# Attention output computed transposed: values as 32-column weights, and no moves or turns of the output

## The chip, the core and the metric

The kernel runs on one NeuronCore of one Trainium2 chip. A core has five engines that run their own instruction streams in order: TensorE (matmuls; PE in the profile, with PEld for its weight loads), VectorE (DVE), ScalarE (ACT), GpSimd (POOL) and SyncE (SP, which here only issues transfers). They meet through semaphores. Matmul results go to PSUM, which has eight banks of 128 partitions by 512 fp32 numbers; everything else lies in SBUF. The metric is the device time of one execution in microseconds (us), the median of several runs.

## What is computed

The input is 2048 tokens of width 448. The block normalizes them, sends the result through two branches and multiplies the branches:

```python
xn = _layernorm(x)                                  # (1, 2048, 448)
q, k, v = split(xn @ wqkv)                          # 16 heads of 28
idx = pos[:, None] - 2 * arange(8)[None, :]         # 8 keys: this token and 7 earlier ones, 2 apart
logits = einsum("bhsd,bhswd->bhsw", q, k[idx]) * 28 ** -0.5   # idx < 0 masked
o = einsum("bhsw,bhswd->bhsd", softmax(logits), v[idx])
s = o.reshape(1, 2048, 448) @ wo
g = silu(gelu(xn @ w1 + b1) @ w2 + b2)              # hidden width 1792
out = x + s * g
```

So there are an attention branch with a short dilated window, a feed-forward branch that serves as a gate, and one multiplication at the end.

## The kernel before

**Layout.** Even and odd tokens are kept apart, which turns the step of 2 into a step of 1: each half is 1024 positions. The 2048 positions stand as 16 tiles of 128 (`t`) and four chunks of 512 (`c`). `xnT` holds the normalized input transposed, four slices of 128 channels each (the last holds 64 channels twice, so that two jobs with only 64 rows of contraction can run side by side in the two halves of the array).

**Projections** (L528, L531 for queries and keys; L554, L557 for values). One tile gives three outputs of 128 x 448 in PSUM, which VectorE or ScalarE cast into `qk_tok` and `v_tok` (L310, L312, one helper for both engines). Heads are padded to 32 columns there. Column 28 and those after it are 1.0 in `v_tok`, so that a product with it also gives the sum of the weights. Queries and keys are transposed by SP's transfers into `qkT`.

**Attention** works in 17 blocks: block 0 has 128 queries, the others have 120, each with 128 keys. Head h is 4g + hl. One PE task (L676) computes the scores of a block: 16 matmuls with 32 rows of contraction each, four of which (hl = 0 to 3) lie in the four row groups of the array and write to four banks. For each hl, ScalarE takes the exponential of a bank into `E` (L682), VectorE multiplies by the mask (L690), and a PE step (L698) multiplies by the values: `E` of four heads as weights of 128 columns, 29 columns of `v` moving. The results of all 16 heads of a block are one bank, with queries on partitions. Values for blocks other than those that start on a tile are moved to partition 0 by GpSimd's transfers (L354, `v<-v_tok`).

**Division and turn.** VectorE inverts the 16 sums (L705) and multiplies (L710) into `os`; GpSimd issues one or two transfers that move the rows of `os` to their place in a tile `ot` (L354, 31 in all); SP issues a transposing transfer per tile (L360, 16 in all) into `oT`, channels on partitions.

**Feed-forward.** L587 and L590 give a 128 x 512 bank of the hidden layer per column tile; ScalarE applies GELU (L594). L627 contracts over 14 tiles of the hidden layer for each token tile. Then come the bias (L649), a tanh (L655) and the gate (L659).

**End** (`final_part`). L740: four matmuls with slices of `oT` as weights and `wo` moving; L745 multiplies by the gate, L750 adds x, and SP writes out.

**What sets the order.** The order on each engine isn't that of the loops. Each piece of work is a task of a `_Plan` with an engine (or two to choose from), an estimated cost, dependencies, buffers to take and give, and a priority out of `PRIO` and `LATER`. The plan is made once in Python by list scheduling, and instructions are then issued in its order; each engine runs its own list strictly in that order. The plan knows three `mode`s of TensorE (128, 64 and 32 rows of contraction), charges 0.095 us (`SWITCH`) for going from one to another, and favours tasks of the small modes while it is in one.

ScalarE has separate function tables for GELU and for exponentials, so the plan does them in stretches: GELU of chunks 0 and 1; exponentials of the blocks of chunks 0 to 2; GELU of chunk 2; exponentials of chunk 3; GELU of chunk 3.

Of the kernel before, what the change touches and what calls it, by code (L numbers as in the profile page):

```python
# [8 lines left out]
F32 = mybir.dt.float32  # L9
BF16 = mybir.dt.bfloat16  # L10
ALU = mybir.AluOpType
# [142 lines left out]
def kernel(  # L154
# [13 lines left out]
    P = 128  # L168
# [64 lines left out]
    def ring(name, n, shape, dt=BF16, fifo=False):  # L233
        return _Pool([sb(f"{name}{i}", shape, dt) for i in range(n)], fifo)

    p_xn = ring("xn", 4, [P, 512])
    p_st = ring("st", 4, [P, 6], F32)
    p_E = ring("E", 8, [P, 4, P], fifo=True)
    p_rd = ring("rd", 2, [P, H], F32)
    p_os = ring("os", 3, [P, D])  # L240
    p_ot = ring("ot", 4, [P, 512])
    p_y = ring("y", 2, [P, D], F32)
    p_t = ring("t", 2, [P, D], F32)
    p_g = ring("g", 4, [P, D])
# [12 lines left out]

    FF1 = (((3, 3), (2, 2), (2, 2)),
           ((2, 4), (2, 2), (2, 2)),
           ((3, 3), (2, 2), (2, 2)),  # L260
           ((5, 3), (3, 3)))
    JOINED = (True, True, False, False)

    PRIO = {
                "project": (47.5, 177.5, 195, 32.5,),
                "project2": (47.5, 147.5, 83, 27,),
                "values": (19.5, 53.5, 102.5, 106.5,),
                "attn": (191.5, 153.5, 199, 129, 79, 74, 54, 45.5, 30.5, 15.5, 15, 5.5, 179, 138.5, 104, 89,
            36.5,),
                "ff1": (170.5, 149, 112, 188, 179, 171.5, 14, 154.5, 143.5, 64, 165.5, 199,),  # L270
                "gelu": (1, 169, 51, 42.5,),
                "ff2": (133.5, 156.5, 162.5, 51.5, 1, 94.5, 109, 5.5, 47, 74.5, 112.5, 31.5, 11.5, 184.5,
            58, 1,),
                "final": (178.5, 32.5, 3, 6, 4, 110, 48.5, 1, 92, 22, 20.5, 50.5, 63, 29, 52.5, 48,),
                "norm": (100.5, 67, 116.5, 168, 199, 166, 159, 131, 1, 130.5, 41, 33, 113, 169, 57.5,
            75.5,),
                "loads": (194.5, 199, 133, 114.5, 69.5,),
                "stats": (83.5, 84, 180.5, 54, 89, 43.5, 2, 115.5, 143, 141.5, 157.5, 148, 29.5, 181, 184,
            81.5,),
                "turn_x": (124, 175, 199, 48, 62, 134, 123, 137, 63, 137, 199, 48.5, 130.5, 159, 35.5,  # L280
            195,),
                "turn_qk": (81.5, 79.5, 61, 171.5, 109, 73.5, 124, 136, 91.5, 31, 33, 153.5, 36.5, 168.5,
            100.5, 24,),
                "turn_o": (1, 1, 129.5, 145.5, 138, 35.5, 137.5, 140.5, 129.5, 20.5, 20.5, 139.5, 199,
            100.5, 42, 57.5,),
                "move_v": (27, 188, 169.5, 91, 52.5, 20, 147, 148.5, 58.5, 114, 93.5, 183.5, 44.5, 57,
            162.5, 175.5, 31,),
                "move_o": (176.5, 1.5, 160.5, 173, 169.5, 165.5, 155, 52.5, 189, 56, 174.5, 118.5, 93, 195,
            135, 163, 128.5,),
                "copies": (33, 125, 87.5, 3, 162, 46, 32, 84, 83.5, 161.5, 58.5, 1.5, 6, 58.5, 167,),  # L290
    }
    LATER = {"qk": 60, "v": 41.5, "gelu": 15, "exp": 35.5, "mask": -30, "pv": -4.5, "recip": 17.5, "os": -17, "y": 7, "tanh": -23, "g": -30, "sg": 9.5, "o": -15.5}

    plan = _Plan()

    def buf(pool, owner, i=0):
        return pool.bufs[owner.slots[pool][i]]
# [4 lines left out]
    def act(n):  # L302
        return 0.15 + n / 1130.0

    def dve(n, r=1):
        return 0.15 + n / (960.0 * r)
# [8 lines left out]
    def memset(eng, ap, v):  # L315
        def fn(_):
            getattr(nc, eng).memset(ap, v)
        return fn
# [17 lines left out]

    t_qz = [plan.add("DVE", 0.08, memset("vector", q[:, :, :, DH:], 0.0), [t_on], prio=95) for q in qk_tok]
    t_vw = [plan.add("DVE", 0.08, memset("vector", v[:, :, DH:], 1.0), [t_on], prio=96) for v in v_tok[:9]]
    t_os = [plan.add("POOL", 0.1, memset("gpsimd", o[:, D:], 0.0), [t_on], prio=94) for o in p_ot.bufs]
    t_row0 = plan.add("POOL", 0.1, memset("gpsimd", row0[:], 0.0), [t_on], prio=93)  # L340
    t_row0 = plan.add("POOL", 0.1, memset("gpsimd", row0[:1, :], 1.0), [t_row0], prio=93)
    t_wo = [plan.add("POOL", 0.45, memset("gpsimd", wo[64:, 3, :], 0.0), [t_on], prio=93)]
    t_E = [plan.add("POOL", 0.1, memset("gpsimd", e[:, :, NQ:], 0.0), [t_on], prio=95) for e in p_E.bufs]

    def dma(eng, dst, src, kb, prio, deps=(), issue=0.5, rate=350.0):
        def fn(_):
# [314 lines left out]
        t_g[t].append(plan.add("DVE", dve(n), f4, [th] + after, prio + LATER["g"], take=(p_g,), give=held + ((p_t, th, 0),)))  # L661


    t_oT, ot_at = {}, {}
    ot = [[] for _ in range(NT)]

    def attn(b, prio, gate, early):
        q0, nq, k0 = BLK[b]
# [11 lines left out]
        for hl in range(4):  # L680
            def f2(k, hl=hl):
                nc.scalar.activation(buf(p_E, k)[:, :, :nq],  # L682
                                     buf(p_b, a, hl)[:, :4 * nq].rearrange("p (g q) -> p g q", g=4),
                                     ACT.Exp, scale=SCALE)
            e = plan.add("ACT", act(4 * nq), f2, [a] + gate + t_E, prio + LATER["exp"], take=(p_E,), give=((p_b, a, hl),), table=("exp",))
            exps.append(e)

            def f3(_, e=e):
                E = buf(p_E, e)
                nc.vector.tensor_tensor(out=E[:, :, :nq], in0=E[:, :, :nq], in1=m[:, :, :nq], op=ALU.mult)  # L690
            w = plan.add("DVE", dve(4 * nq, 2), f3, [e] + t_mask, prio + LATER["mask"])

            def f4(k, e=e, hl=hl):
                ps = buf(p_b, pv[0] if hl else k)[:].rearrange("p (h c) -> p h c", h=H)
                v = buf(*v_at[b]) if v_at[b] else v_tok[k0 // P]
                for g in range(G):
                    h = 4 * g + hl
                    nc.tensor.matmul(ps[:, h, :DH + 1], buf(p_E, e)[:, g, :], v[:, h, :DH + 1],  # L698
                                     start=True, stop=True)
            pv.append(plan.add("PE", 0.12, f4, [w] + t_v[b] + pv[-1:], prio + LATER["pv"], take=() if hl else (p_b,),  # L700
                               give=((p_E, e, 0),) + ((v_at[b],) if hl == 3 and v_at[b] else ()), tail=0.15))
        po = pv[0]

        def f5(k):
            nc.vector.reciprocal(buf(p_rd, k)[:nq, :],  # L705
                                 buf(p_b, po)[:nq, :].rearrange("p (h c) -> p h c", h=H)[:, :, DH])
        r = plan.add("DVE", 0.25, f5, [pv[-1]], prio + LATER["recip"], take=(p_rd,))

        def f6(k):
            nc.vector.tensor_tensor(  # L710
                out=buf(p_os, k)[:nq, :].rearrange("p (h c) -> p h c", h=H),
                in0=buf(p_b, po)[:nq, :].rearrange("p (h c) -> p h c", h=H)[:, :, :DH],
                in1=buf(p_rd, r)[:nq, :].unsqueeze(2).to_broadcast((nq, H, DH)), op=ALU.mult)
        o = plan.add("DVE", dve(D), f6, [r], prio + LATER["os"], take=(p_os,), give=((p_b, po, 0), (p_rd, r, 0)))
        q, mine = q0, []
        while q < q0 + nq:
            t, row = divmod(q, P)
            n = min(P - row, q0 + nq - q)
            first, d = dma_sb(lambda k, t=t, row=row, n=n: buf(p_ot, ot_at.get(t, k))[row:row + n, :D],
                          lambda q=q, n=n: buf(p_os, o)[q - q0:q - q0 + n, :], [o] + t_os + mine + [d for _, d in ot[t]],  # L720
                          PRIO["move_o"][b], () if ot[t] else (p_ot,), ((p_os, o, 0),) if q + n == q0 + nq else ())
            ot[t].append((first, d))
            mine = [first]
            ot_at[t] = ot[t][0][0]
            if row + n == P:
                t_oT[t] = dma_T(oT[:, :, t * P:(t + 1) * P], lambda t=t: buf(p_ot, ot_at[t])[:], [d for _, d in ot[t]], PRIO["turn_o"][t],
                                (p_ot, ot_at[t], 0))
            q += n
        return exps


# [4 lines left out]
    def final_part(t, cs, n, g, prio):  # L736
        def f1(k):
            ps = buf(p_b, k)
            for kt in range(KT):
                nc.tensor.matmul(ps[:, :n], oT[:, kt, t * P:(t + 1) * P], wo[:, kt, cs],  # L740
                                 start=(kt == 0), stop=(kt == KT - 1))
        a = plan.add("PE", pe(n, KT), f1, [t_oT[t]] + t_wo + [t_f2[t]], prio, take=(p_b,), tail=0.15)

        def f2(k):
            nc.vector.scalar_tensor_tensor(out=buf(p_sg, k)[:, :n], in0=buf(p_b, a)[:, :n], scalar=0.5,  # L745
# [1 line left out]
        s = plan.add("DVE", dve(n), f2, [a, g], prio + LATER["sg"], take=(p_sg,), give=((p_b, a, 0), (p_g, g, 0)))  # L747

        def f3(k):
            nc.vector.tensor_tensor(out=buf(p_o, k)[:, :n], in0=x_sb[:, t, cs], in1=buf(p_sg, s)[:, :n], op=ALU.add)  # L750
        o = plan.add("DVE", dve(n, 2), f3, [s], prio + LATER["o"], take=(p_o,), give=((p_sg, s, 0),))

        def f4(_):
            nc.sync.dma_start(rows(o_half, t * P, P)[:, cs], buf(p_o, o)[:, :n])
# [47 lines left out]
    def project(c):  # L802
# [19 lines left out]
        for b in blocks_of[c]:  # L822
# [12 lines left out]
    t_w2 = [[dma("SP", w2[:, 7 * i:7 * i + 7, :], B_w2[F // 2 * i:F // 2 * (i + 1), :].rearrange("(m p) c -> p m c", p=P),  # L835
                 784, PRIO["loads"][4], turned, 1.0)] for i in range(2)]
    t_b2 = dma("POOL", b2[:], B_b2.rearrange("(o d) -> o d", o=1).to_broadcast((P, D)), 112, 82, turned)
    t_wo += [dma("POOL", wo[:, 0:3, :], ktiles(A_wo[0:KF, :]), 336, 80, [t_w2[1][0]]),
             dma("POOL", wo[:64, 3, :], A_wo[KF:D, :], 56, 79, [t_w2[1][0]])]
    for t in range(2 * TPC, NT):  # L840
        stats(t)
        if t % TPC == TPC - 1:
# [61 lines left out]
```

## Time and profile before

| | us |
|---|---|
| median of 7 runs | 161.62 |
| lowest and highest | 160.78, 163.58 |
| the profiled execution | 161.63 |
| its span, first to last instruction | 159.9 |

The span is 1.7 us shorter than the time of the same execution; the rest lies around the program.

| engine | busy, us | instructions |
|---|---|---|
| TensorE | 154.2 | 1309 |
| VectorE | 104.6 | 278 |
| ScalarE | 100.2 | 184 |
| GpSimd | 44.5 | 104 |

How to read the profile. A line of groups gives the source line, the engine, the operation, output and inputs by name, the shape, how many there were, then busy time and mean duration of one, then the time the engine was idle just before them and what ended it. Matmuls are pipelined: the recorded duration of one is longer than the time until the next can start, so the price of a matmul is the distance between starts. The timeline merges neighbours of one line into a piece with its start and its length; from the start of one piece to the start of the next is what it took. The mean granted clock of TensorE was 1.000.

### The profile page before, as it was taken

The page shows a single profiled execution, that of the slowest core. Times are in us where ns is not written, and L with a number is a line of the kernel's source. Part 1 is how long each engine was busy: PE and PEld are TensorE (multiplying, and loading weights), DVE is VectorE, ACT ScalarE, POOL GpSimd, SP SyncE. Part 2 cuts the span into 40 slices and gives each one's busy share as a digit, 9 for nine tenths or more (in the row PEclk, how much of TensorE's full clock was granted, in tenths as well). Part 3 has the DMA queues.
Part 4 walks back from the last instruction along what each step waited for, and adds up shares of the span by engine and source line. Part 5 has one row for each costly group of instructions (what it writes and reads, how often), then busy time and mean ns, then how long its engine had stood idle before and what let it go on. Part 6 is the DMA issues. An engine that isn't in the chain of part 4 may idle for free.

```text
span 159.9 us, 3581 instructions
## 1 busy us (share of the span) xinstructions
PE 154.2 (96%) x1309; PEld 76.6 (48%) x1309; DVE 104.6 (65%) x278; ACT 100.2 (63%) x184; POOL 44.5 (28%) x104
## 2 busy tenths in 40 slices
PE   6999999999999999999999999999999999999990
PEld 2744334443445555444654555335556544445580
DVE  4786540695549788666698989703988990604972
ACT  3256497677667865863856767866987659552030
POOL 7404350254601244030474554010522220000000
PEclk9999999999999999999999999999999999999999
DMA  5999898999991794281695999730344431021021
GB/s 145 321 297 265 98 208 127 372 321 219 133 176 25 66 215 107 49 174 50 89 165 124 171 221 185 51 76 0 105 90 101 64 88 33 29 60 33 31 86 29
DMA packets 42941, 20.80 MB, mean 130 GB/s; under 512 B 34160, under 2 KB 41476, under 8 KB 42924
## 3 DMA queue, kind: packets, MB, share of 16 engines
q1 hardware_dynamic: 40252, 16.14, 51.4%
q0 software_dynamic: 2528, 4.32, 12.9%
q8 instruction: 10, 0.16, 0.4%
q10 hardware_dynamic: 144, 0.11, 0.3%
q14 instruction: 7, 0.06, 0.1%
HBM read 7.06 MB, written 1.84 MB: 56 GB/s over the span
## 4 chain that ended last, share of the span: by engine, by line
PE 83%; DMA 8%; SPq 2%; ACT 2%; issue 1%; DVE 1%; ACTq 0%; DVEq 0%
PE bank L627 25%; PE bank L587 21%; PE bank L528 9%; PE bank L740 7%; DMA b1T<-b1r 5%; PE bank L554 5%; PE bank L698 5%; PE bank L590 4%; PE bank L676 3%; DMA w_in<-in_A_wqkv_dram 3%; SPq L347 2%; PE bank L531 2%; PE bank L557 1%; ACT L594 1%; ACT E L682 1%
## 5 line engine op out<-in xcount | busy, mean ns | idle before, releaser
L627 PE MATMUL bank<-w,h 128*128 128x448 bf16 (+1 forms) x238 | 46.1, 342 | 0.0
L594 ACT ACTIVATE h<-bank,b 128x512 bf16<-128x512 f32 x56 | 34.0, 694 | 10.7 <-PE bank L590 6.6
L682 ACT ACTIVATE E<-bank 128x480 bf16<-128x480 f32 (+1 forms) x68 | 33.8, 581 | 10.7 <-PE bank L676 9.6
L587 PE MATMUL bank<-xnT,w 128*128 128x512 bf16 x168 | 39.6, 380 | 0.1
L627 PEld LDWEIGHTS <-h 128*128 128x128 bf16 x238 | 22.0, 97 | 17.3
L354 POOL DMA_DIRECT2D ot<-os x31 | 16.5, 536 | 45.8 <-DVE os L710 28.3
L354 POOL DMA_DIRECT2D v<-v_tok x30 | 16.4, 549 | 44.6 <-ACT v_tok L310 16.5
L587 PEld LDWEIGHTS <-w 128*128 128x128 bf16 x168 | 15.5, 98 | 21.8 <-issue 5.1
L528 PE MATMUL bank<-w_in,xnT 128*128 128x448 bf16 x96 | 22.2, 353 | 0.0
L690 DVE TENSOR_TENSOR E<-E,m_gen 128x480 bf16<-128x480 bf16 x60 | 21.2, 400 | 0.8 <-ACT E L682 0.7
L655 ACT ACTIVATE t<-y 128x448 f32<-128x448 f32 x15 | 8.8, 585 | 13.2 <-DVE y L649 13.2
L649 DVE TENSOR_TENSOR y<-bank,b 128x448 f32<-128x448 f32 x15 | 9.3, 623 | 10.1 <-PE bank L627 9.7
L740 PE MATMUL bank<-wo,oT 128*128 128x448 bf16 (+1 forms) x68 | 14.2, 341 | 0.0
L312 DVE CAST qk_tok<-bank 128x448 bf16<-128x448 f32 x13 | 8.0, 617 | 8.2 <-PE bank L528 7.8
L698 PEld LDWEIGHTS <-E 128*128 128x128 bf16 x272 | 10.6, 96 | 5.8 <-issue 0.9
L310 ACT CAST qk_tok<-bank 128x448 bf16<-128x448 f32 x19 | 9.8, 535 | 4.9 <-PE bank L528 2.7
L554 PE MATMUL bank<-w_in,xnT 128*128 128x448 bf16 x48 | 11.7, 353 | 0.0
L528 PEld LDWEIGHTS <-xnT 128*128 128x128 bf16 x96 | 8.0, 97 | 7.6 <-issue 1.5
L403 DVE BATCH_NORM_STATS2 st<-x_sb 128x6 f32<-128x448 bf16 x16 | 9.7, 606 | 2.6 <-DMA x_sb<-in_A_x_dram 2.6
L745 DVE SCALAR_TENSOR_TENSOR sg<-bank,g 128x448 bf16<-128x448 f32 x9 | 5.6, 623 | 8.3 <-ACT h L594 7.2
L710 DVE TENSOR_TENSOR os<-bank,rd 120x448 bf16<-120x448 f32 (+1 forms) x17 | 10.5, 620 | 0.5
L698 PE MATMUL bank<-v,E 128*128 128x29 bf16 x240 | 10.2, 176 | 0.0
(67 smaller groups left out, 132.5 us busy)
## 6 DMA issues: line engine op xcount, KB each, us to landing
out_dram<-o SPq DMA_DIRECT2D x15, 112.0 KB, 1.7
w<-in_B_w_dram SPq DMA_DIRECT2D x2, 784.0 KB, 7.4
w<-in_B_w_dram SPq DMA_DIRECT2D x2, 672.0 KB, 8.2
x_sb<-in_A_x_dram SPq DMA_DIRECT2D x3, 448.0 KB, 6.1
w_in<-in_A_wqkv_dram SPq DMA_DIRECT2D x3, 336.0 KB, 3.8
w<-in_B_w_dram SPq DMA_DIRECT2D x4, 112.0 KB, 7.9
wo<-in_A_wo_dram POOLq DMA_DIRECT2D x1, 336.0 KB, 4.6
qkT<-qk_tok SPq DMA_TRANSPOSE x16, 5.0
```

The source lines that it names most:

```text
L310: nc.scalar.copy(o, i)
L354: nc.gpsimd.dma_start(dst(k), src())
L528: nc.tensor.matmul(ps[:, :D], xnT[:, kt, cs], w_in[:, kt, which * D:(which + 1) * D], start=start, stop=stop)
L554: nc.tensor.matmul(ps[:, :D], xnT[:, kt, k0:k0 + P], w_in[:, kt, 2 * D:], start=start, stop=stop)
L587: nc.tensor.matmul(ps[:], w1[:, kt, ms], xnT[:, kt, cs], start=start, stop=stop)
L594: nc.scalar.activation(buf(p_h, own, i)[:], buf(p_b, own, i)[:], ACT.Gelu_apprx_tanh, bias=b1[:, mt:mt + 1])
L627: nc.tensor.matmul(ps[:, :n], buf(*h_at[(c, mt)])[:, j * P:(j + 1) * P], w2[:, mt, cs], start=(mt == 0 and not biased), stop=(mt == NMT - 1))
L682: nc.scalar.activation(buf(p_E, k)[:, :, :nq], buf(p_b, a, hl)[:, :4 * nq].rearrange("p (g q) -> p g q", g=4), ACT.Exp, scale=SCALE)
L690: nc.vector.tensor_tensor(out=E[:, :, :nq], in0=E[:, :, :nq], in1=m[:, :, :nq], op=ALU.mult)
L698: nc.tensor.matmul(ps[:, h, :DH + 1], buf(p_E, e)[:, g, :], v[:, h, :DH + 1], start=True, stop=True)
L710: nc.vector.tensor_tensor(out=buf(p_os, k)[:nq, :].rearrange("p (h c) -> p h c", h=H), in0=buf(p_b, po)[:nq, :].rearrange("p (h c) -> p h ...
L740: nc.tensor.matmul(ps[:, :n], oT[:, kt, t * P:(t + 1) * P], wo[:, kt, cs], start=(kt == 0), stop=(kt == KT - 1))
```

## The change

1. **P V.** Where a step had `E` as weights and 29 columns of values moving, it now has the values of one head as weights (128 keys, 32 columns: 28 channels, and four columns of 1.0) and `E` moving (120 queries). Head 4g + hl goes to partitions 32g to 32g + 31 and to columns hl·nq onward of the bank. The four matmuls of a step lie in the four column groups of the array. The plan's cost of a step goes from 0.12 to 0.065, and its `mode` stays 128. The number of matmuls, 272, is the same.
2. **Division.** The bank now has channels on partitions, and rows 28 to 31 of each group of 32 hold the sums of that head, for each query. VectorE transposes the bank in blocks of 32 x 32 into `dt` (fp32), inverts one column of each block, transposes the inverses back, spread over 32 columns, and multiplies the bank by them, straight into `oT`.
3. **Gone:** `os`, `ot`, the 31 moves, the 16 transposing transfers of the output, and the memsets of `ot` and of the last columns of `E`.
4. **`wo`** is laid out to match: four transfers of 28 rows each, into an area that is first zeroed as a whole.
5. **The last addition** (`o`) of the first eight tiles may go to GpSimd.
6. **Plan:** new priorities, and another grouping of the hidden layer's tiles (`FF1`): 11 batches before, 12 after.

```diff
-           ((3, 3), (2, 2), (2, 2)),
-           ((5, 3), (3, 3)))
+           ((2, 4), (2, 2), (2, 2)),
+           ((2, 2), (2, 2), (2, 4)))
...
-    t_wo = [plan.add("POOL", 0.45, memset("gpsimd", wo[64:, 3, :], 0.0), [t_on], prio=93)]
-    t_E = [plan.add("POOL", 0.1, memset("gpsimd", e[:, :, NQ:], 0.0), [t_on], prio=95) for e in p_E.bufs]
+    t_wo = [plan.add("POOL", 1.0, memset("gpsimd", wo[:], 0.0), [t_on], prio=93)]
...
             def f4(k, e=e, hl=hl):
-                ps = buf(p_b, pv[0] if hl else k)[:].rearrange("p (h c) -> p h c", h=H)
                 v = buf(*v_at[b]) if v_at[b] else v_tok[k0 // P]
                 for g in range(G):
-                    h = 4 * g + hl
-                    nc.tensor.matmul(ps[:, h, :DH + 1], buf(p_E, e)[:, g, :], v[:, h, :DH + 1],
-                                     start=True, stop=True)
-            pv.append(plan.add("PE", 0.12, f4, [w] + t_v[b] + pv[-1:], prio + LATER["pv"], take=() if hl else (p_b,),
+                    nc.tensor.matmul(buf(p_b, pv[0] if hl else k)[32 * g:32 * g + 32, hl * nq:(hl + 1) * nq],
+                                     v[:, 4 * g + hl, :], buf(p_E, e)[:, g, :nq], start=True, stop=True)
+            pv.append(plan.add("PE", 0.065, f4, [w] + t_v[b] + pv[-1:], prio + LATER["pv"], take=() if hl else (p_b,),
...
         def f5(k):
-            nc.vector.reciprocal(buf(p_rd, k)[:nq, :],
-                                 buf(p_b, po)[:nq, :].rearrange("p (h c) -> p h c", h=H)[:, :, DH])
+            nc.vector.transpose(buf(p_dt, k)[:, :4 * nq], buf(p_b, po)[:, :4 * nq])
...
         def f6(k):
-            nc.vector.tensor_tensor(
-                out=buf(p_os, k)[:nq, :].rearrange("p (h c) -> p h c", h=H),
-                in0=buf(p_b, po)[:nq, :].rearrange("p (h c) -> p h c", h=H)[:, :, :DH],
-                in1=buf(p_rd, r)[:nq, :].unsqueeze(2).to_broadcast((nq, H, DH)), op=ALU.mult)
...
-            first, d = dma_sb(lambda k, t=t, row=row, n=n: buf(p_ot, ot_at.get(t, k))[row:row + n, :D],
...
-                t_oT[t] = dma_T(oT[:, :, t * P:(t + 1) * P], lambda t=t: buf(p_ot, ot_at[t])[:], [d for _, d in ot[t]], PRIO["turn_o"][t],
...
+            nc.vector.reciprocal(buf(p_rd, k)[:, :nq // 8],
+                                 buf(p_dt, d)[:, :4 * nq].rearrange("p (b c) -> p b c", c=32)[:, :, DH])
...
+        def f7(_):
+            nc.vector.transpose(buf(p_dt, d)[:, :4 * nq].rearrange("p (b c) -> p b c", c=32),
+                                buf(p_rd, r)[:, :nq // 8].unsqueeze(2).to_broadcast((P, nq // 8, 32)))
...
+        def f8(_):
+            nc.vector.tensor_tensor(out=oT[:, :, q0:q0 + nq],
+                                    in0=buf(p_b, po)[:, :4 * nq].rearrange("p (l q) -> p l q", l=4),
+                                    in1=buf(p_dt, d)[:, :4 * nq].rearrange("p (l q) -> p l q", l=4), op=ALU.mult)
...
-        o = plan.add("DVE", dve(n, 2), f3, [s], prio + LATER["o"], take=(p_o,), give=((p_sg, s, 0),))
+        o = plan.add(("DVE", "POOL") if t < 2 * TPC else "DVE", (dve(n, 2), 1.15) if t < 2 * TPC else dve(n, 2), f3, [s], prio + LATER["o"], take=(p_o,), give=((p_sg, s, 0),))
...
-    t_wo += [dma("POOL", wo[:, 0:3, :], ktiles(A_wo[0:KF, :]), 336, 80, [t_w2[1][0]]),
-             dma("POOL", wo[:64, 3, :], A_wo[KF:D, :], 56, 79, [t_w2[1][0]])]
+    t_wo += [dma("POOL", wo[32 * g:32 * g + 28, :, :], A_wo[112 * g:112 * g + 112, :].rearrange("(l c) d -> c l d", l=4),
+                 100, 80, [t_w2[1][0]] + t_wo[:1]) for g in range(G)]
```

## Prediction

> **What bounds the kernel now.** I read the page's busy times and slices first, then the chain of waits, then TensorE's timeline, because only the timeline tells whether a "busy" TensorE moves at its own pace.
>
> ```profile
> PE 154.2 (96%) x1309; PEld 76.6 (48%) x1309; DVE 104.6 (65%) x278; ACT 100.2 (63%) x184; POOL 44.5 (28%) x104
> ...
> PE   6999999999999999999999999999999999999990
> ...
> DVE  4786540695549788666698989703988990604972
> ...
> PE 83%; DMA 8%; SPq 2%; ACT 2%; issue 1%; DVE 1%; ACTq 0%; DVEq 0%
> ```
>
> TensorE is busy in every slice but the last, and the chain that ended last runs 83% through it. VectorE has slices of 8 and 9 only where attention runs.
>
> ```profile
> 61.09 0.55 PE L698 MATMUL bank<-v,E 128*128 128x29 bf16 x16
> 61.50 1.29 PE L554 MATMUL bank<-w_in,xnT 128*128 128x448 bf16 x6
> 62.72 0.55 PE L557 MATMUL bank<-w_in,xnT 64*128 64x448 bf16 x4
> 63.21 0.39 PE L676 MATMUL bank<-qkT 32*128 32x120 bf16 x16
> 63.53 0.74 PE L554 MATMUL bank<-w_in,xnT 128*128 128x448 bf16 x3
> ...
> 76.16 1.31 PE L528 MATMUL bank<-w_in,xnT 128*128 128x448 bf16 x6
> 77.30 0.95 PE L698 MATMUL bank<-v,E 128*128 128x29 bf16 x32
> 78.11 2.24 PE L627 MATMUL bank<-w,h 128*128 128x448 bf16 x11
> ```
>
> From start to start: six 448-column matmuls take 77.30 - 76.16 = 1.14, so 0.19 each: there is no gap. 32 matmuls of P V take 78.11 - 77.30 = 0.81, so 0.025 each and 0.10 per step of four. The same six followed by 64-row work take 62.72 - 61.50 = 1.22: going to another array mode costs about 0.09. The 16 score matmuls take 63.53 - 63.21 = 0.32. Their rounds of four run side by side; with one more switch of 0.09 to 0.11 behind them, a round of 120 columns is 0.0525. In the trace's single records the four of a round start 4 ns apart, and at each of these switches the weight load too starts only about 0.09 after the stream before it has ended. I use 0.093 per switch. Adding such prices over TensorE's list from the first projection (7.07) to the last matmul's end (155.27) gives 146.7 against 148.2 passed, and single gaps over 0.04 beyond the price come to only 0.65. So after 7 us the time is TensorE's list, and an edit is worth what it does to that list, unless another engine comes late.
>
> ```profile
> L690 DVE TENSOR_TENSOR E<-E,m_gen 128x480 bf16<-128x480 bf16 x60 | 21.2, 400 | 0.8 <-ACT E L682 0.7
> L710 DVE TENSOR_TENSOR os<-bank,rd 120x448 bf16<-120x448 f32 x16 | 9.9, 620 | 0.5
> L649 DVE TENSOR_TENSOR y<-bank,b 128x448 f32<-128x448 f32 x15 | 9.3, 623 | 10.1 <-PE bank L627 9.7
> L705 DVE RECIPROCAL rd<-bank 120x16 f32<-120x16 f32 x16 | 4.0, 252 | 3.0 <-PE bank L698 3.0
> ...
> 70.00:98.00 28.00, 27.98 (x337) 15.00 (x336) 22.58 (x53) 18.32 (x38) 13.20 (x25) 1.00 0.81 145
> ...
> 113.00:128.00 15.00, 15.00 (x206) 8.74 (x206) 13.33 (x34) 11.76 (x24) 5.29 (x10) 1.00 0.42 88
> ```
>
> The last two lines are windows: length, then busy time of PE, PEld, DVE, ACT, POOL. VectorE was busy 13.33 of 15.00, 89%, from 113 to 128, and TensorE still didn't pause. In the first group 60 x 0.400 is 24.0 but busy is 21.2: instructions back to back overlap by 0.047 each.
>
> **What the Trainium skill says.** "TensorEngine Tiling (Array Packing)", Key Properties: "Changing tiling mode (not just tile) drains the TensorE", and its list of modes has 128x32 beside 128x128; the 0.09 above agrees for changes of rows, and nothing in this trace shows a change of columns alone. The same page, Restrictions: column tiling disables fast weight load. "TensorE: Matmul & The Clock Gate", Measured speedup: three column tiles gave 2.38x, so they do run side by side; here only row tiles show it. "Vector Engine (DVE) Microarchitecture Reference", 3.8: the 32x32 transpose sustains one element per cycle per lane; no row here shows one.
>
> **The change, part by part**, by the order of the changed program's instructions.
>
> *P V itself.* Before: 272 x 0.0254 = 6.9. After: 68 steps, which stand in 37 runs; 68 x 0.0525 + 37 x 0.012 (three starts 4 ns apart) = 4.0. That is -2.9. Bounds: 68 x 0.0525 = 3.6 if every run overlaps perfectly; without fast load the page's columns/1.2 ns (section LDWEIGHTS) gives 27 ns per load of 32 columns, and four in series 0.107, so 7.3, or +0.4. I take 4.0, because score loads hid under their streams.
>
> *Switches.* Before, TensorE's list changes mode 73 times. After, without counting P V as a mode, 78: one more feed-forward batch, and fewer places where tails and scores lie side by side. That is 5 x 0.093 = +0.5. If 32 columns are a mode of their own, the 37 runs have 74 borders; 20 of them face scores or 64-row tails, where a switch is due anyway, and 54 are new: 54 x 0.093 = +5.0. The plan leaves P V at mode 128, so nothing gathers these steps: 21 of the 37 runs are one step of four. Bounds: 0 and 5.0. I take 5.0, by the page, and because the switches that the trace does show all cost this, between whatever two row modes.
>
> *VectorE.* Removed: 17 x (0.252 + 0.620) = 14.8. Added per block of 480 columns: both transposes and the product at one fp32 element per cycle. Row L649 gives 0.623 for 448, so 0.66 for 480; the inverse stays 0.25: 3 x 0.66 + 0.25 = 2.23, times 17 = 37.9. Five additions go to GpSimd (17 to 12): -1.9. ScalarE takes over 13 casts (VectorE has 9 instead of 22, counting those of xnT): -8.0. Busy: 104.6 + 37.9 - 14.8 - 9.9 = 117.8, and ScalarE 100.2 + 13 x 0.537 = 107.2. Neither passes TensorE in sum; the dense stretch decides. From the last mask of block 0 to that of block 9 VectorE's list has 36 masks (14.4), 8 sets of four (17.8), 5 y, 6 g and 5 sg (16 x 0.62 = 9.9), 3 casts (1.9) and one o (0.4): 44.4, less 88 x 0.047 for overlap = 40.3. TensorE's list between the P V steps behind those masks is 47.6 with the switches and 44.7 without. That is 85% or 90%, as in the window at 89% that held nothing up. The first transpose of a block waits for its last P V step, and behind it in VectorE's list stand masks that TensorE's next steps wait for; the inverse stood there before, with 3.0 of idle time ahead of it (L705) and no harm. I add 0.2 for waits; bounds 0 and 3.
>
> *Transfers.* 31 moves (0.54 of GpSimd each) and 16 turns (1.2 of SP each) go, and with them the 2.4 and 3.2 to landing between `os` and `oT`. TensorE waited 0.2 for `oT` in all, so it's worth nothing, though finals may now be placed earlier. In exchange the product of a block keeps its bank for 2.2 instead of 0.9 after P V.
>
> *GpSimd, `wo`, head and tail.* Zeroing `wo` whole is 1792/448 x 0.466 = 1.9 against 0.47, but 0.94 of memsets of `E` and `ot` go. The masks end near 6.7 instead of 6.2, and VectorE copies them at 9.75. `wo`'s four transfers stand where the two stood at 42, and the first final comes some 12 us after scores begin at 44.5. An addition on GpSimd (the plan's 1.15; 0.384 on VectorE) feeds only an output transfer. TensorE's list up to the feed-forward and the end after its last matmul (4.6) are the same: nothing.
>
> **Sum.** -2.9 + 0.5 + 5.0 + 0.2 = +2.8. The profiled execution took 161.63 (span 159.9), the median is 161.62, so no correction: 164.4.
>
> **Rivals.**
>
> *Columns don't drain.* With rows left at 128, the array might take the next weights in the background. Then -2.9 + 0.5, and 0 to 1 of waits, since VectorE is then at 90%: 159.2 to 160.2. For it: nothing here shows a switch of columns. Against: the page's sentence, which excepts no mode.
>
> *Half a drain.* 54 x 0.045 = 2.4 cancels the gain: -2.9 + 0.5 + 2.4 leaves 161.6, no change.
>
> *VectorE becomes the bound*, on the slow side too. The slack in the stretch is 47.6 - 40.3 = 7.3 over 32 new instructions: 0.23 each. If an fp32 transpose takes two cycles per element, it is 1.16, and 16 of them add 8.0: 0.7 too much there, with every wait between PE and VectorE exposed, and the same again for blocks 12 to 15. I put that at +2 each on top of the switches: 168. Against: the page's one element per cycle. It decides from about 1.1 per transpose on (7.3/16 over 0.66), and costs something before that.
>
> **How the numbers follow.** Drain 0.50 (163.4 to 166.8: waits and loads upward, runs that overlap better downward); no drain 0.34; half 0.09; VectorE bound 0.07. The range must reach both sides: 158.8 to 166.8, with the rest above and a little below. Within 0.5% (160.8 to 162.4, about what can't be told from no change) lie most of the half drain and the edges of the first two: 0.11; faster 0.33, slower 0.56.
>
> **What would show it.** In the timeline of after, a wide group before a P V run takes 0.09 longer to the next start than the same group before wide work, and the run 0.06 + 0.09: drain. If four narrow matmuls follow within 0.01 and the run costs 0.065, none. Transposes should read 0.63 to 0.70, VectorE near 118 busy, its dense slices at 9. If gaps before P V or scores that VectorE ended sum to over 1 us, my tally of the stretch was wrong; if TensorE's list without gaps isn't near 149, the switches were.

## The result, and the profile after

| | before | after |
|---|---|---|
| median, us | 161.66 (31 runs) | 164.19 (12 runs) |
| lowest and highest, us | 160.58, 165.11 | 163.58, 165.84 |
| ratio, 95% interval | | 1.0166 [1.0138, 1.0194] |

The change costs 2.5 us. The profiled execution of the changed kernel took 165.36, with a span of 163.7; it holds a wait early on, shown below, that the traces of other kernels with the same order don't have. The ratios here and below leave out executions more than 1.5% above the fastest of the same kernel, four of the 31 here.

The page's busy times, TensorE's and VectorE's slices and the shares of the chain, after:

```profile
PE 157.0 (96%) x1309; PEld 71.0 (43%) x1309; DVE 118.5 (72%) x294; ACT 106.7 (65%) x197; POOL 34.7 (21%) x68
...
PE   6999799999999999999999999999999999999990
...
DVE  4896420657298599889768978966879879619972
...
PE 81%; DMA 12%; SPq 2%; DVE 2%; POOL 1%; issue 1%; DVEq 0%
```

TensorE is still busy in nearly every slice (the first and the last aside, only the fifth reads 7), the chain still runs 81% through it, and VectorE has 14 us more work. These totals say little about the loss, since TensorE's busy share is 96% in both. TensorE's timeline of after says it (start, length, what, how many):

```profile
61.06 1.50 PE L619 MATMUL bank<-w,h 128*128 128x448 bf16 x7
62.49 0.34 PE L687 MATMUL bank<-E,v 128*32 128x120 bf16 x12
62.76 0.74 PE L546 MATMUL bank<-w_in,xnT 128*128 128x448 bf16 x3
63.43 0.24 PE L687 MATMUL bank<-E,v 128*32 128x120 bf16 x4
63.60 0.74 PE L546 MATMUL bank<-w_in,xnT 128*128 128x448 bf16 x3
...
108.88 0.39 PE L687 MATMUL bank<-E,v 128*32 128x120 bf16 x16
109.21 1.47 PE L579 MATMUL bank<-xnT,w 128*128 128x512 bf16 x6
```

Seven matmuls at 0.189 are 1.32, but the next start comes after 62.49 - 61.06 = 1.43. Three are 0.57, and 63.43 - 62.76 is 0.67. So the wide group in front pays 0.10 when P V follows. The lone step of four takes 63.60 - 63.43 = 0.17, where a step of the kernel before took 0.10. Sixteen in one run take 0.33, four rounds and one switch. Single records confirm it: 0.283 instead of 0.189 from the last wide start to P V, and from the last P V start to wide work 0.158 after a lone step, 0.148 after a longer run, instead of 0.053.

VectorE's new work in the groups of after, and P V's weight loads (busy, mean ns, then idle time before and its cause):

```profile
L696 DVE STREAM_TRANSPOSE dt<-bank 128x480 f32<-128x480 f32 (+1 forms) x17 | 11.6, 682 | 13.6 <-PE bank L687 13.5
L705 DVE STREAM_TRANSPOSE dt<-rd 128x480 f32<-128x480 f32 (+1 forms) x17 | 11.6, 680 | 0.6
L710 DVE TENSOR_TENSOR oT<-bank,dt 128x480 bf16<-128x480 f32 (+1 forms) x17 | 11.2, 657 | 0.5
L687 PEld LDWEIGHTS <-v 128*32 128x32 bf16 x240 | 4.4, 94 | 11.1 <-issue 10.5
```

Both transposes take 0.68, near the 0.66 expected. VectorE idles 13.5 in all before the first of them, waiting for P V; that is harmless here, because TensorE doesn't wait for VectorE anywhere in attention (the records below show no such gap over 0.04).

From the single records I split TensorE's time from the start of the first 448-column projection to the start of the last matmul. The distance between two starts, less the price of the first (columns / 2.4 + 2.5 ns, which gives the 0.189 and 0.216 that the trace shows; for the 29 columns of the kernel before the 25 ns of its trace), is counted as a mode change where the mode differs. It counts as a wait where it exceeds the price by over 0.04 without a change; at a change, an excess over 0.2 leaves 0.095 to the change and the remainder to the wait.

| kernel | passed, us | mode changes | their cost | waits | the rest |
|---|---|---|---|---|---|
| before | 148.31 | 73 | 6.81 | 0.56 | 140.94 |
| after | 152.65 | 132 | 12.61 | 1.59 | 138.45 |
| e1_wide | 145.54 | 78 | 7.35 | 0.53 | 137.66 |
| e2_nodiv | 151.51 | 132 | 12.62 | 0.57 | 138.32 |
| e4_twice | 155.51 | 132 | 12.83 | 4.18 | 138.50 |
| e5_block | 157.14 | 103 | 9.78 | 8.99 | 138.37 |
| e6_block_plan | 147.38 | 92 | 8.63 | 0.83 | 137.92 |
| e7_pair_plan | 148.82 | 107 | 10.06 | 0.57 | 138.19 |
| e8_step_plan | 150.92 | 112 | 10.66 | 2.10 | 138.16 |

The rest became 2.5 less, the 59 added mode changes cost 5.8, and 1.0 is more waiting. Split by matmul, the records say more: P V's own part of the rest falls from 6.98 to 4.12, by 2.9, while that of the 128 x 128 work grows by 0.4. In every mode the first matmul after a change, or the first round of matmuls side by side, takes 0.010 longer than those behind it (0.200 instead of 0.189 for 448 columns, 0.063 instead of 0.053 for a round of 120), and after has 28 returns to 128 x 128 work more than before; that is 0.3 of the 0.4. So the added changes cost about 6.1, a little over 0.10 each. All the waiting of after lies in its first 27 us. Its timeline there:

```profile
17.27 2.12 PE L579 MATMUL bank<-xnT,w 128*128 128x512 bf16 x9
20.46 1.46 PE L579 MATMUL bank<-xnT,w 128*128 128x512 bf16 x6 [1.08 <-ACT h L586]
```

Nine matmuls at 0.216 would let the next start at 19.2; it starts at 20.46, because the GELU behind it waited for its bias, which VectorE could convert only at 18.18, when its transfer had landed. e2_nodiv (the experiments follow below) has the same order here and its bias at 16.83, and its timeline runs through:

```profile
17.86 3.41 PE L579 MATMUL bank<-xnT,w 128*128 128x512 bf16 x15
```

15 matmuls take 21.20 - 17.86 = 3.34 there (the next piece starts at 21.20), with no gap. So this wait belongs to one execution; what is left of the list's growth are the mode changes.

### The profile page after: what moved, and what is told of

Read it like the earlier page. It is cut to its first block, busy times and chain, and to the rows that moved or that the text cites. A ratio compares the mean times of both kernels' runs of the same rounds, so it can differ in the third digit from the quotient of the medians.

```text
span 163.7 us, 3483 instructions
## 1 busy us (share of the span) xinstructions
PE 157.0 (96%) x1309; PEld 71.0 (43%) x1309; DVE 118.5 (72%) x294; ACT 106.7 (65%) x197; POOL 34.7 (21%) x68
## 4 chain that ended last, share of the span: by engine, by line
PE 81%; DMA 12%; SPq 2%; DVE 2%; POOL 1%; issue 1%; DVEq 0%
PE bank L619 27%; PE bank L579 18%; PE bank L520 10%; PE bank L727 8%; DMA b1T<-b1r 5%; PE bank L546 5%; PE bank L687 5%; DMA w_in<-in_A_wqkv_dram 3%; DMA xnT<-xn 3%; PE bank L582 3%; PE bank L667 3%; SPq L339 2%; PE bank L523 2%; PE bank L549 1%; POOL rstd L417 1%
## 5 line engine op out<-in xcount | busy, mean ns | idle before, releaser
L619 PE MATMUL bank<-w,h 128*128 128x448 bf16 (+1 forms) x238 | 46.7, 342 | 0.0
L673 ACT ACTIVATE E<-bank 128x480 bf16<-128x480 f32 (+1 forms) x68 | 33.8, 577 | 15.8 <-PE bank L667 13.5
L681 DVE TENSOR_TENSOR E<-E,m_gen 128x480 bf16<-128x480 bf16 x60 | 21.8, 414 | 0.8 <-ACT E L673 0.7
L520 PE MATMUL bank<-w_in,xnT 128*128 128x448 bf16 x96 | 22.3, 354 | 0.1
L696 DVE STREAM_TRANSPOSE dt<-bank 128x480 f32<-128x480 f32 (+1 forms) x17 | 11.6, 682 | 13.6 <-PE bank L687 13.5
L304 ACT CAST qk_tok<-bank 128x448 bf16<-128x448 f32 x27 | 13.5, 541 | 3.7 <-PE bank L523 1.6
L546 PE MATMUL bank<-w_in,xnT 128*128 128x448 bf16 x48 | 12.1, 354 | 0.0
L705 DVE STREAM_TRANSPOSE dt<-rd 128x480 f32<-128x480 f32 (+1 forms) x17 | 11.6, 680 | 0.6
L710 DVE TENSOR_TENSOR oT<-bank,dt 128x480 bf16<-128x480 f32 (+1 forms) x17 | 11.2, 657 | 0.5
L429 DVE TENSOR_SCALAR xn<-x_sb,mv,rstd 128x448 bf16<-128x448 bf16 x16 | 6.4, 401 | 6.1 <-DMA xnT<-xn 4.0
L687 PE MATMUL bank<-E,v 128*32 128x120 bf16 x240 | 9.6, 222 | 0.0
L687 PEld LDWEIGHTS <-v 128*32 128x32 bf16 x240 | 4.4, 94 | 11.1 <-issue 10.5
```

Of the source, the lines that this page charges most:

```text
L304: nc.scalar.copy(o, i)
L520: nc.tensor.matmul(ps[:, :D], xnT[:, kt, cs], w_in[:, kt, which * D:(which + 1) * D], start=start, stop=stop)
L546: nc.tensor.matmul(ps[:, :D], xnT[:, kt, k0:k0 + P], w_in[:, kt, 2 * D:], start=start, stop=stop)
L619: nc.tensor.matmul(ps[:, :n], buf(*h_at[(c, mt)])[:, j * P:(j + 1) * P], w2[:, mt, cs], start=(mt == 0 and not biased), stop=(mt == NMT - 1))
L673: nc.scalar.activation(buf(p_E, k)[:, :, :nq], buf(p_b, a, hl)[:, :4 * nq].rearrange("p (g q) -> p g q", g=4), ACT.Exp, scale=SCALE)
L687: nc.tensor.matmul(buf(p_b, pv[0] if hl else k)[32 * g:32 * g + 32, hl * nq:(hl + 1) * nq], v[:, 4 * g + hl, :], buf(p_E, e)[:, g, :nq], s ...
```

## The experiments

The theory: 32 columns are an array mode of their own, and the 54 new changes between it and 128 x 128 work are the loss. Rivals: VectorE's four instructions per block, or the transfers that went.

**e1_wide: no 32-column mode.** Each step of four is one matmul with 128 columns of values as weights. It leaves out three of the four heads' products in each step.

```diff
-                for g in range(G):
-                    nc.tensor.matmul(buf(p_b, pv[0] if hl else k)[32 * g:32 * g + 32, hl * nq:(hl + 1) * nq],
-                                     v[:, 4 * g + hl, :], buf(p_E, e)[:, g, :nq], start=True, stop=True)
+                nc.tensor.matmul(buf(p_b, pv[0] if hl else k)[:, hl * nq:(hl + 1) * nq],
+                                 v[:, 4 * hl:4 * hl + 4, :].rearrange("p g c -> p (g c)"),
+                                 buf(p_E, e)[:, 0, :nq], start=True, stop=True)
```

> The changed kernel with one matmul per P V step instead of four: 128 columns of values (four neighbouring heads) as weights, the E of one head moving. It leaves out three quarters of P V, so the output is not the reference's. The streaming time of a step stays one round of 120 columns (0.0525 us) and the order of every engine stays, but TensorE never enters a 32-column mode. Theory (the loss is 54 added mode switches of 0.093): TensorE's list loses 54 x 0.093 = 5.0 and the 37 x 0.012 of staggered starts, 0.4, so about 158.8 against 164.2 for the changed kernel, up to 159.8 if VectorE then holds it up. Rival (VectorE's longer chain is the loss): unchanged, 163.5 or more, since VectorE's work is untouched.

158.71, ratio to before 0.9841 [0.9815, 0.9866]; just below the expectation. TensorE's timeline:

```profile
59.07 0.23 PE L686 MATMUL bank<-E,v 128*128 128x120 bf16 x1
59.13 1.49 PE L619 MATMUL bank<-w,h 128*128 128x448 bf16 x7
60.46 0.37 PE L686 MATMUL bank<-E,v 128*128 128x120 bf16 x3
```

A step costs 0.06, and the seven wide matmuls before P V take 1.33, 0.19 each: the 0.10 ahead of P V is gone, while VectorE's instructions are the same. In the table 54 mode changes fewer are 5.3 us less, 0.097 each. The edit also takes away three quarters of P V's matmuls and weight loads; but in the changed kernel a round of four of them inside a run takes 0.053, no more than the step here, so it isn't they that cost.

**e2_nodiv and e3_wide_nodiv: no division.** Both transposes and the inverse are left out, and the product is a copy of the bank into `oT`; the division by the sums is missing. e2 does this to the changed kernel, e3 to e1_wide as well.

```diff
-            nc.vector.transpose(buf(p_dt, k)[:, :4 * nq], buf(p_b, po)[:, :4 * nq])
+            pass
...
-            nc.vector.tensor_tensor(out=oT[:, :, q0:q0 + nq],
-                                    in0=buf(p_b, po)[:, :4 * nq].rearrange("p (l q) -> p l q", l=4),
-                                    in1=buf(p_dt, d)[:, :4 * nq].rearrange("p (l q) -> p l q", l=4), op=ALU.mult)
+            nc.vector.tensor_copy(oT[:, :, q0:q0 + nq],
+                                  buf(p_b, po)[:, :4 * nq].rearrange("p (l q) -> p l q", l=4))
```

> The changed kernel without both transposes and the inverse of each block; the product is a copy out of the bank. It leaves out the division by the sums. VectorE loses 17 x (0.680 + 0.250 + 0.680) = 27 us of work, TensorE's order and switches stay. Theory (switches): the time stays at 164.2, within 0.7. Rival (VectorE): back to 161.7 or below, since VectorE then has less to do than before the change.

> Both edits at once: one wide matmul per P V step, and no division (three quarters of P V and the division are left out). Theory: 158.8, the same as the first edit alone or less by the waits that VectorE causes once TensorE's list is shorter (0 to 1.0). Rival (VectorE): this alone is clearly faster than the first edit, by 2 or more.

e2: 164.33, ratio 1.0187 [1.0164, 1.0209]; e3: 158.21, 0.9811 [0.9784, 0.9838]. VectorE's busy time fell from 118.5 to 94.3, and the time didn't move. Beside e1_wide, without the 32-column mode, leaving the division out saves 0.5, with ratios whose intervals overlap. The division isn't what made the change slow.

**e4_twice: VectorE's slack.** The first transpose of each block is done twice, 17 x 0.68 = 11.6 us of work more.

```diff
             nc.vector.transpose(buf(p_dt, k)[:, :4 * nq], buf(p_b, po)[:, :4 * nq])
+            nc.vector.transpose(buf(p_dt, k)[:, :4 * nq], buf(p_b, po)[:, :4 * nq])
```

> The changed kernel with the first transpose of each block done twice (the same result). VectorE gains 17 x 0.680 = 11.6 us. From the last mask of block 0 to that of block 9 the tally left VectorE 7.3 us of slack, and this adds 8 x 0.68 = 5.4 there. Theory: 0 to 1.0 slower than the changed kernel, 164.2 to 165.2. Rival (VectorE is already the bound there): 5 or more slower.

A miss: 169.42, ratio 1.0504 [1.048, 1.0528], 5.2 over the changed kernel. VectorE's timeline, and below it TensorE's at the same place:

```profile
86.21 0.68 DVE L696 STREAM_TRANSPOSE dt<-bank 128x480 f32<-128x480 f32 x1 [1.31 <-PE bank L687]
86.93 0.68 DVE L697 STREAM_TRANSPOSE dt<-bank 128x480 f32<-128x480 f32 x1
...
88.65 0.66 DVE L711 TENSOR_TENSOR oT<-bank,dt 128x480 bf16<-128x480 f32 x1
89.22 1.35 DVE L681 TENSOR_TENSOR E<-E,m_gen 128x480 bf16<-128x480 bf16 x4
```

```profile
88.40 0.73 PE L520 MATMUL bank<-w_in,xnT 128*128 128x448 bf16 x3
89.77 0.24 PE L687 MATMUL bank<-E,v 128*32 128x120 bf16 x4 [0.64 <-DVE E L681]
```

VectorE first stands idle for 1.31, since its next instruction is the transpose that needs a whole block of P V. Then it works through the block's chain, and only behind it come the masks that TensorE needs: TensorE waits 0.64. The stretch from the last mask of block 0 to that of block 9 (start and end, length, then busy time of PE, PEld, DVE, ACT, POOL) in e4_twice and, in the second fence, in after:

```profile
47.40:99.20 51.80, 49.50 (x515) 21.98 (x508) 46.66 (x97) 34.49 (x72) 13.48 (x21) 1.00 0.52 86
```

```profile
48.60:97.20 48.60, 48.60 (x515) 21.74 (x508) 41.33 (x88) 34.40 (x72) 13.43 (x21) 1.00 0.51 91
```

With the same 515 matmuls the stretch is 3.2 us longer, though VectorE still idles 51.80 - 46.66 = 5.1 us in it. Slack in an engine that runs its list strictly in order is not a reserve that any instruction may draw on. The division is free in the changed kernel, but 0.68 more per block in this place isn't.

**e5_block: all of P V at once, same priorities.** The plan gets a fourth mode for P V, favours only tasks of the mode that it is in, and has one P V task of 16 matmuls per block.

```diff
-            pv.append(plan.add("PE", 0.065, f4, [w] + t_v[b] + pv[-1:], prio + LATER["pv"], take=() if hl else (p_b,),
-                               give=((p_E, e, 0),) + ((v_at[b],) if hl == 3 and v_at[b] else ()), tail=0.15))
...
+        pv.append(plan.add("PE", 0.222, f4, ws + t_v[b], prio + LATER["pv"], take=(p_b,),
+                           give=tuple((p_E, e, 0) for e in es) + ((v_at[b],) if v_at[b] else ()), tail=0.15, mode=33))
```

> All 16 matmuls of a key block's P V are one task of the planner, in a mode of their own, with the priorities as they were. The order then has 103 mode switches and 17 runs of P V in place of 132 and 37. If the drained array is the whole cost of the change and nothing else gets in the way: 164.2 - 29 x 0.093 - 20 x 0.012 = 161.3. Rival: VectorE's order and the eight buffers of E are close to being the bound, so a P V that has to wait for all four masks of its block, and holds four buffers until then, leaves TensorE waiting; one wait of 0.3 in each of 17 blocks is +5, so 164 to 168, with gaps beyond price in TensorE's timeline in the attention that the changed kernel doesn't have.

171.95, ratio 1.0619 [1.0552, 1.0685]: the rival, and more of it. TensorE's timeline:

```profile
100.62 0.24 PE L691 MATMUL bank<-E,v 128*32 128x120 bf16 x4
101.68 0.24 PE L691 MATMUL bank<-E,v 128*32 128x120 bf16 x4 [0.82 <-DVE E L681]
103.29 0.24 PE L691 MATMUL bank<-E,v 128*32 128x120 bf16 x4 [1.37 <-DVE E L681]
```

Mode changes fell to 103 and 9.8 us, but the waits are 9.0: with the old priorities a block's P V is issued before its masks are through, and TensorE stops inside it.

**e6_block_plan, e7_pair_plan, e8_step_plan: the order chosen anew.** The priorities and the groups of the hidden layer were searched for again with the plan's own costs, P V having its own mode: one task per block (e6), per two steps (e7), per step (e8). The matmuls are the same in all, but besides the size of the P V task the whole order differs, and so do the groups (10, 11 and 9 batches, 12 in after). The shape of the edit, from e8 (the tasks of e6 are as in e5):

```diff
-            at, t, e, c = min(near, key=lambda k: (-k[1].prio - (TILED if tiled and k[1].mode != 128 else 0), k[0], k[1].seq))
+            at, t, e, c = min(near, key=lambda k: (-k[1].prio - (TILED if tiled and k[1].mode == self.mode else 0), k[0], k[1].seq))
...
-                               give=((p_E, e, 0),) + ((v_at[b],) if hl == 3 and v_at[b] else ()), tail=0.15))
+                               give=((p_E, e, 0),) + ((v_at[b],) if hl == 3 and v_at[b] else ()), tail=0.15, mode=33))
```

> The same one task for each key block, with the planner's priorities and the groups of the first feed-forward product chosen anew for it. 92 mode switches and 15 runs of P V. Drained array only: 164.2 - 40 x 0.093 - 22 x 0.012 = 160.2, which would be below the kernel before (161.5). Rival (VectorE's order as in the expectation before): gaps of 2 us and more in TensorE's timeline and 162 or more.

> P V in tasks of two steps (eight heads), in a mode of their own, priorities chosen anew. 107 mode switches and 24 runs of P V. Drained array only: 164.2 - 25 x 0.093 - 13 x 0.012 = 161.7. If instead the new priorities do the work and the number of switches does nothing, it stands with e6_block_plan and e8_step_plan at one time.

> P V in single steps as in the changed kernel; the planner is only told that their mode isn't that of the scores, and its priorities are chosen anew. 112 mode switches and 30 runs of P V. Drained array only: 164.2 - 20 x 0.093 - 7 x 0.012 = 162.3. If new priorities by themselves were the gain, it would be as fast as e6_block_plan.

| | mode changes | expected | measured | ratio to before |
|---|---|---|---|---|
| e6_block_plan | 92 | 160.2 | 160.35 | 0.9926 [0.9904, 0.9948] |
| e7_pair_plan | 107 | 161.7 | 162.39 | 1.0053 [1.0023, 1.0083] |
| e8_step_plan | 112 | 162.3 | 164.46 | 1.0179 [1.0124, 1.0234] |

e6 came out as worked out, and it is faster than both kernels. e7 is 0.7 late. e8 missed by 2.2: its profiled execution has 2.1 us of waits, more than half of them within or before P V, and took 163.32, while the other executions reach 165.14 and aren't in the trace. e6's page, timeline, and a window as long as that of after:

```profile
PE 153.1 (96%) x1309; PEld 72.1 (45%) x1309; DVE 119.6 (75%) x293; ACT 105.8 (67%) x196; POOL 36.9 (23%) x70
```

```profile
65.11 0.39 PE L681 MATMUL bank<-E,v 128*32 128x120 bf16 x16
65.44 0.39 PE L657 MATMUL bank<-qkT 32*128 32x120 bf16 x16
65.76 1.50 PE L609 MATMUL bank<-w,h 128*128 128x448 bf16 x7
```

```profile
48.60:97.20 48.60, 48.44 (x543) 22.77 (x542) 45.50 (x96) 37.82 (x80) 15.64 (x24) 1.00 0.57 96
```

P V of a block takes 0.33, and with scores right behind it three changes do for both. VectorE is busy 45.50 of 48.60 here, 94%, more than the 46.66 of 51.80, 90%, of e4_twice, and TensorE is idle for only 0.16. So a high busy share of VectorE alone doesn't make TensorE wait; in e4 it was where the work stood in VectorE's list.

**e10_before_plan: is it the search?** The kernel before, with its own tasks and modes, searched in the same way; only the numbers in `PRIO`, `LATER` and the groups (`FF1`, 10 batches) differ, such as

```diff
-    LATER = {"qk": 60, "v": 41.5, "gelu": 15, "exp": 35.5, "mask": -30, "pv": -4.5, "recip": 17.5, "os": -17, "y": 7, "tanh": -23, "g": -30, "sg": 9.5, "o": -15.5}
+    LATER = {"qk": 51.9, "v": 60, "gelu": 60, "exp": 60, "mask": -30, "pv": 60, "recip": 5.9, "os": 8.6, "y": 42.5, "tanh": -30, "g": 13.7, "sg": -30, "o": 19.5}
```

> The kernel before with its planner's priorities searched for again in the same way and as long as those of e6_block_plan. 72 mode switches for 73. If e6_block_plan is faster because of its fewer switches and shorter P V: 161.4, within 0.5. If a new search by itself is worth a microsecond: 160.5.

162.24, ratio 1.006 [1.0033, 1.0087]: this new search of the kernel before gains nothing on the chip, and even loses a little. So e6's gain isn't that of a search alone.

**e12_block_other: another order of the same kind.** As e6, with another result of the search:

```diff
-    p_E = ring("E", 8, [P, 4, P], fifo=True)
+    p_E = ring("E", 10, [P, 4, P], fifo=True)
```

> The one task for each key block again, with ten buffers of E for eight and another result of the search for priorities: 94 mode switches and 15 runs of P V. Drained array only: 164.2 - 38 x 0.093 - 22 x 0.012 = 160.4, so the time of e6_block_plan within 0.5. If e6_block_plan owes its time to its one order and not to the number of switches: 162 or more.

161.89 in four executions, from 160.16 to 162.91, where the kernel before took 162.63 on the same chip. The ratio, 0.9897 [0.9803, 0.9992], rests on the two fastest alone; the medians are 0.5% apart. In the profiled execution, which took 162.56, TensorE stands for 2.2 us in the middle of a block's scores, until VectorE's `y` is through. So this run settles neither side of its expectation: e6 is the only complete kernel here that is clearly faster than the kernel before.

**e9_moves and e11_moves_two: the transfers back.** Moves and turns like those of the kernel before are issued again after each block, with data that nothing reads. e9 has one buffer for the moved rows, e11 two.

```diff
+            first, dd = dma_sb(lambda k, t=t, row=row, n=n: buf(p_ot, ot_at.get(t, k))[row:row + n, :D].rearrange("p (l c) -> p l c", l=4),
+                          lambda q=q, n=n: oT[q - q0:q - q0 + n, :, q0:q0 + 112], [o] + t_os + mine + [d for _, d in ot[t]],
...
+                dma_T(spare[:], lambda t=t: buf(p_ot, ot_at[t])[:], [d for _, d in ot[t]], PRIO["turn_o"][t],
```

> The changed kernel, to which 31 moves on GpSimd's queue and 16 turns on SyncE's are added again, as many and as large as in the kernel before and issued after the same blocks; what they carry is the new output of a block, and nothing reads it. TensorE's order is the changed kernel's. If the transfers were hidden in the kernel before and their loss is worth nothing: 164.2, within 0.5. Rival: they held up other transfers on the two queues, and taking them away was a gain that the mode switches ate: then 165 or more, with gaps at TensorE that end in a transfer.

> As e9_moves, with two buffers for the moved rows in place of one (the turned copy goes over a mask that is no longer needed), so that the added transfers needn't wait for each other until after the last matmul. If the transfers are hidden while TensorE works and only their own queue made e9_moves late: 164.2, within 0.5, and TensorE's first projection to last matmul as in the changed kernel. Rival: the queues are the reason, and it stays above 170.

e9: 190.64, ratio 1.1739 [1.1668, 1.1811], a miss by 26. TensorE's slices on its page, and a line of its waits (total, times, longest):

```profile
PE   7999999999999999999999999999999995000000
```

```profile
POOL ot L353 <- DMA spare<-ot: 72.3, 14, 11.0
```

TensorE went through its list as before: 151.0 from the first projection to the last matmul, after which its slices read 0. What came late were the added transfers themselves: each move waits for the turn that frees the one buffer, 72.3 us in all, and the last ends 31 us after the last matmul, where the changed kernel ends 4.5 after it. With two buffers e11 took 165.03 where the kernel before took 162.63 on that chip, ratio 1.0171 [1.0098, 1.0244], the same as the change's 1.0166; first projection to last matmul is 151.4. In after it is 152.65, of which 1.24 are the wait in the head, so the list takes the same 151.4. Thus the added transfers are hidden, and taking them away is worth nothing that shows (the interval of the times leaves room for 1.2 us). Nothing reads them here; in the kernel before, where the final product did, TensorE waited 0.2 for `oT` in all.

## Why the prediction was right

**The likeliest case was the one that happened**: 164.4 forecast, 164.19 measured. The Trainium skill, "TensorEngine Tiling (Array Packing)", Key Properties, says that a change of mode drains the array, and after and e1_wide show that a change of columns costs what one of rows does. They show this price, not what the array does meanwhile.

**Switches, +5.5 (5 + 54 at 0.093).** 132 changes as counted; 12.61 - 6.81 = 5.8 by the records, so 0.3 more, and another 0.3 stands in the first wide matmuls behind the changes. The price of a change was forecast at 0.093 and is a little over 0.10 with the slower first matmul behind it, which the forecast left out. So the lone step, forecast at 0.06 + 0.09, took 0.17, and the wide group ahead of it 0.10 instead of 0.09.

**P V, -2.9.** Measured -2.9, 6.98 - 4.12. Behind the first round of a run the rounds take the forecast 0.0525. The other end of the bound (0.107 per step, loads in series) is excluded: 16 matmuls and their switch in 0.33 leave no room for 16 loads at the forecast's estimate of 27 ns, 0.43. The same page of the skill, Restrictions, says that column tiling disables the fast load; no cost of that shows in this kernel, since the rounds of the scores, whose loads have 128 columns, take 0.0525 too.

**Waits, +0.2.** None in attention; the 1.0 of the table lies in the head of one execution. Together the list grew by 3.3 without its waits (-2.9, +5.8, +0.4) and not by 2.6: the price of a switch was the term that was too small, their number was right. That the total still fits is partly chance, since the first projection starts at 6.49 instead of 7.07, and over the kernels with that order this start varies between 6.49 and 7.04. (The forecast read the list of before 0.1 short: its last matmul starts at 155.38, so 148.3 passed, not 148.2.)

**VectorE.** 118.5 for 117.8 and 106.7 for ScalarE's 107.2; transposes 0.680 for 0.66. What failed is what the rival makes of the slack: "The slack in the stretch is 47.6 - 40.3 = 7.3 over 32 new instructions". The sum itself came out, 48.60 - 41.33 = 7.3 in after. But e4_twice adds 8 x 0.68 = 5.4 in that stretch, less than 7.3, and the stretch still grows by 3.2, the whole kernel by 5.2. A difference of sums over 48 us isn't what decides; a wait is decided instruction by instruction: what stands behind a block's transposes, and who needs it.

**Transfers, head and tail at nothing.** e11 bears out the transfers. The changes on GpSimd and to `wo` weren't tried alone; no wait of TensorE in the trace of after ends in them. That the first projection starts up to 0.6 earlier in that order wasn't forecast.

**Rivals.** "Columns don't drain" gave 159.2 to 160.2; e1_wide, which has no column mode, shows that this price was about right for a kernel without the drain (158.7, with a quarter of the P V). The idea behind the change thus holds: P V is 2.9 cheaper, and in one order with the steps together it wins (e6, 0.9926), though 19 changes more than before remain.

## What to carry to other kernels

Before splitting a matmul into tiles of another shape, count the borders that its steps get in the final order and multiply by the price of a change that the trace shows (0.10 here): short steps of 0.06 scattered among wide work pay three times their own length. Tell the scheduler that the shape is a mode, then gather the steps and choose the order again, since merging alone (e5) turned mode changes into waits. And don't measure an in-order engine's reserve by its busy share: look at what is queued behind the instruction that grows.

## What was not expected of the hardware

- A change of columns alone (128 x 128 to 128 x 32) costs 0.094 going in and 0.096 coming out, no less than a change of rows (0.09 to 0.096).
- In each of the four modes the first matmul or round after a change takes 0.010 longer than the next: 0.200 instead of 0.189, 0.063 instead of 0.053. A lone P V step therefore costs 0.106 coming out.
- The loads of 32 columns hide in a run: rounds of four at 0.053, as with the scores.
- A 32 x 32 block transpose of 128 x 480 fp32 takes 0.680 from PSUM and 0.678 from SBUF, 1.42 ns per column, hardly more than the product of that size (0.655).
